# Delta rule and MLP on one core: chunks 2 and 3 from 32-token rows, and TensorE's small products regrouped

## The chip, the cores and the metric

The kernel runs on one core of a Trainium2 chip. The metric is the device time of one execution in microseconds (us), the median of three runs for the kernel before. A profiled execution gives a trace of every engine: TensorE (PE, with its weight loads PEld), VectorE (DVE), ScalarE (ACT), GpSimd (POOL) and SyncE (SP), and of the DMA queues. All inputs and results are fp32, but for the two weight matrices, which lie in DRAM as 64-bit numbers and are converted on the core.

## What is computed

A delta-rule attention over 4 batches, 8 heads, 768 tokens and head size 48, followed by layer norm and a two-layer MLP with a residual:

```python
def _attn_ref(q, k, v, beta):
    k_n = k / (np.linalg.norm(k, axis=-1, keepdims=True) + 1e-06)
    state = np.zeros((B, H, D, D)); y = np.zeros_like(q)
    for t in range(S):
        kt, vt, bt = k_n[:, :, t], v[:, :, t], beta[:, :, t, None]
        y[:, :, t] = np.einsum('bhd,bhde->bhe', q[:, :, t], state)
        v_old = np.einsum('bhde,bhd->bhe', state, kt)
        state = state + bt[..., None] * np.einsum('bhd,bhe->bhde', kt, vt - v_old)
    return y

def _moe_ref(x, g_ln, w_ch1, w_ch2):        # x: (4, 768, 384)
    mu, var = mean(x), mean((x - mu) ** 2)
    xn = (x - mu) / np.sqrt(var + 1e-06) * g_ln
    return x + np.maximum(xn @ w_ch1, 0.0) @ w_ch2    # 384 -> 1536 -> 384
```

## The kernel before

**Chunks.** The 768 tokens are cut into 12 chunks of 64 (`C`), and each chunk treats all 32 pairs of batch and head at once: two batches' halves on the partitions (`e`), heads in the columns. For a chunk the kernel forms the keys turned (`first_kt` by TensorE transposes, or `load_blocks` and `turned`, a DMA in blocks and a VectorE transpose), the Gram matrix of the keys (`gram`, or `gram_queries` together with the products of keys and queries), the inverse of a unit triangular matrix made from it and beta, and then `recur`: `ks` and `qs` (state times keys and queries), `u` (the inverse applied to v minus `ks`), the state's update `s`, the output `y`, layer norm, and x turned to `xnt` for the MLP.

**Inverses.** VectorE inverts by rows: step j multiplies a column by a row and subtracts (two instructions for each j). `rows_near` does this for blocks of 16 tokens (15 steps): once for chunk 0 alone and once for chunks 1 and 2 together, `rows_near((1, 2))`. From two 16-token blocks `near_join` makes the inverse of a 32-token block (two groups of TensorE products, E and Z, with copies between), and `join` makes the inverse of all 64 tokens from two of 32 (again two groups, e and z). So u of chunks 0, 1 and 2 is one product with a 64-token inverse (L1147, L1177). From chunk 3 `rows_inverse(m)` inverts 32-token blocks on VectorE (31 steps, L1058 and L1065) for the pair of chunks 2m+1 and 2m+2 (3 and 4 first), and u is formed in three steps (L1166): the first 32 tokens' inverse on v, the off-diagonal block of the Gram matrix (`goff`) on that u, subtracted from v on VectorE (L1170), and the second inverse.

**MLP.** `mlp(c)` multiplies chunk c's 256 rows with the two weight matrices. Chunks 0 to 2 use plain products for the first layer (L1447), chunk 0 also for the second (L1469); the others use sums of blocks that need fewer products (`eleven` with L1380 and sums on VectorE, `seven` with L1548 and sums on GpSimd). These products are the large ones; all others above are small and come in groups of 32 or 64.

**Buffers.** The eight banks of PSUM are `two` and `by` (two banks each, for the small products) and `f0` to `f3` (the MLP; at the start also the small ones). Chunk 0's and 1's q, gram and joins use several buffers of their own (`kt3`, `qt1`, `xn1`, `xt1`).

**Order.** All instructions are first entered as steps with an engine, an estimated cost and their inputs. `Line.schedule` plays the program through with these costs, picks for each engine the next step by priority (due times `DUE`, caps `CAP`, earliest times `T0`), and `emit` writes the instructions in the order of the planned starts, which `in_this_order` fixes for each engine and for the DMA issues. So a change of a cost or of these tables moves the whole order. `pe_time` holds what the plan believes of TensorE: a pass's cost (`PASS`), a cost for going between large and small products (`SWITCH`), 128 passes per block of instructions (`BLOCK`, `FETCH`), and a clock that depends on earlier windows (`WINDOW`, `WARM`). `warm_up` puts products with zeros (L1632) into TensorE's planned idle time until the MLP begins.

Of the kernel before, what the change touches and what calls it, by code (L numbers as in the profile page):

```python
# [65 lines left out]
PASS = 0.0165  # L66


class Step:
    __slots__ = (  # L70
        "eng", "cost", "fn", "deps", "pr", "lag", "bulk", "start", "end", "n", "users", "name", "t0", "np", "arr", "hold", "ready", "least", "due", "port", "banks", "cap", "pk"
# [3 lines left out]
class Line:  # L75
# [6 lines left out]
    PE_TAIL, SWITCH, OVERLAP = 0.12, 0.1, 0.1  # L82
    BLOCK, FIRST, FETCH = 128, 93, 3.95
    WINDOW, WARM, KEEP = 3.413, 0.44, 0.6
    DMA_ISSUE, DMA_DONE, LANES = 1.4, 1.0, 8

    def __init__(self):
        self.steps = []
        self.filler, self.fill_after, self.fills = None, (), []
        self.writer = {}  # L90
        self.readers = {}

    def add(self, eng, cost, fn, r=(), w=(), pr=0.0, lag=0.0, bulk=None, name="", t0=0.7, after=(), np=0, arr=0.0, hold=None, due=None, port=0, cap=None, pk=16.0):
        s = Step()
        s.eng, s.cost, s.fn, s.pr, s.lag, s.bulk, s.name, s.t0 = eng, cost, fn, pr, lag, bulk, name, t0
        s.np, s.arr, s.n = np, arr, len(self.steps)
        s.hold, s.due, s.cap, s.pk = False, due, cap, pk
# [15 lines left out]
        deps.discard(s)  # L113
        s.deps = sorted(deps, key=lambda d: d.n)
# [9 lines left out]

    def pe_time(self, s, t, commit):
        passes, bi, begun, wins = self.passes, self.block, self.begun, self.wins
        if self.big != (s.due is not None):
            t += self.SWITCH
        left, stall, new = max(s.np, 1), 0.0, {}
        per = s.cost / left  # L130
        while left:
# [9 lines left out]
            warm = wins.get(w - 1, 0.0) + new.get(w - 1, 0.0) >= self.WARM * self.WINDOW  # L141
            f = 1.0 if warm else 2.0
# [3 lines left out]
            new[w] = new.get(w, 0.0) + m * per  # L146
            t += m * max(per, f * min(per, self.wide(s)))
            passes += m
            left -= m
        if commit:  # L150
            self.big = s.due is not None
            self.passes, self.block, self.begun = passes, bi, begun
            for w, a in new.items():
                wins[w] = wins.get(w, 0.0) + a
        return t, stall

    def warm_up(self, t, until):
# [3 lines left out]
        while t + cost + 0.2 < until:  # L161
            w = int(t / self.WINDOW)
            if self.wins.get(w, 0.0) > self.KEEP * (t + cost - w * self.WINDOW):
                t = t + 0.1
                continue
# [47 lines left out]
    def offer(self, u):  # L213
        t = u.t0
        for d in u.deps:
            t = max(t, d.end + (self.NEXT if d.eng == u.eng and d.bulk is None else self.HOP))
        u.ready = t + u.lag
        self.avail[u.eng].append((u.ready, u))

    def foresee(self, now):  # L220

        soon, ends = {e: [] for e in ENGS}, {}
        for s in self.held:
# [5 lines left out]
            for d in s.deps:  # L229
                z = d.end if d.end is not None else ends.get(d, max(now, self.free[d.eng]) + d.cost)  # L230
                t = max(t, z + (self.NEXT if d.eng == s.eng and d.bulk is None else self.HOP))
# [4 lines left out]
    def run(self):  # L236
# [3 lines left out]
        self.passes, self.block, self.begun, self.wins = 0, 0, 0.7, {}  # L240
        self.big = False
# [42 lines left out]
        while todo:  # L284
# [29 lines left out]
            if any(r < t and h.start is None and h.pr < pick.pr for r, h in self.soon[e]):  # L314
                self.foresee(t)
            first = [max(r, t + 0.05) for r, h in self.soon[e] if h.start is None and h.pr < pick.pr]
            if first and t + pick.cost > first[0] + self.GIVE and waits.get(e, 0) < self.PATIENCE:
# [26 lines left out]
            if e == "PE":  # L344
                if self.filler and not self.big and self.fill_after and all(x.start is not None and x.end <= free[e] for x in self.fill_after):
                    self.warm_up(free[e], t)
# [14 lines left out]
    def schedule(self):  # L361
# [5 lines left out]
        for s in reversed(every):  # L367
# [4 lines left out]
            if s.due is None:  # L372
                s.pr -= self.EAGER * (s.eng == "PE")
        goal = min((s for s in every if s.due is not None), key=lambda s: s.due)
# [28 lines left out]
def kernel(  # L403
# [23 lines left out]
    NSL = (NCH - 1 + SLAB - 1) // SLAB  # L427
# [5 lines left out]
    NP = H // 2  # L433
    TURNED = 4
    LNPE = 2
# [9 lines left out]
    def sb(name, shape, dt=FP32):  # L445
# [21 lines left out]
    xn1, xt1 = sb("xn1", [128, GH, C]), sb("xt1", [128, GH, C])  # L467
    kts = [kq[:, 0] for kq in kqs] + [sb("kt3", [128, GH, C])]
    qts = [kqs[0][:, 1], sb("qt1", [128, GH, C]), kqs[1][:, 1], kqs[2][:, 1]]
    pts = [sb(f"pt{i}", [128, GH, C]) for i in range(2)] + [xn1, xt1]  # L470
# [3 lines left out]
    xts = [xt0, xt1, kqs[1][:, 1], xt3]  # L474
# [10 lines left out]
    xnjs = [  # L485
        t.rearrange("p h t -> p (h t)").rearrange("p (c h t) -> p c h t", c=SLAB, t=BK) for t in (kqs[2][:, 1], xn1)
    ]
# [8 lines left out]
    xor, bits, ma, mb_ = (small[:, n].bitcast(I32) for n in range(4))  # L496
    mask4 = sb("mask4", [128, BK], I32)
    lane = sb("lane", [128, 3])
    beta_s = sb("beta_s", [128, 1 + SLAB, FB])
# [5 lines left out]
    second = [t.rearrange("p h t -> p (h t)") for t in (qts[1], pts[1])]  # L505
# [5 lines left out]
    knrm = sb("knrm", [128, GH])  # L511
# [3 lines left out]
    two = psum.tile([128, 2, 512], FP32, name="two")  # L515
    by = psum.tile([128, 2, 512], FP32, name="by")
    f_ = [psum.tile([128, 512], FP32, name=f"f{i}") for i in range(4)]
# [3 lines left out]
    DUE = [427.765, 583.601, 213.154, 268.307, 795.608, 269, 907.321, 333.938, 602.225, 394.884, 1217.56, 1460.55, 0.099, 0, 1.793, 59.617]  # L521
    CAP = [700.448, 198.32, 1075.41, 558.357, 371.457, 461.226, 203.442, 537.048, 455.27, 590.32, 447.02, 315.018, 444.4, 322.431, 447.17, 466.169, 726.277]
    T0 = [18.636, 10.706, 30.485, 64.109, 123.03, 38.361, 76.47, 154.521, 173.066, 81.563, 50.167, 32.713, 40.943, 38.356, 19.795, 25.96, 3.78, 24.511, 36.996, 21.431, 91.901, 74.05]
# [18 lines left out]
    def one_of(c):  # L542

        return c % 2 if c < 3 else (0, 0, 2, 3)[c - 3 if c < 4 else 1 + (c - 4) % 3]

    def kt_of(c):
        return c if c < 4 else (c - 4) % 3
# [18 lines left out]
    def dma(eng, out_, in_, n, ns, r=(), w=(), **kw):  # L566

        cost = 0.65 if eng == "Pool" else 0.39 if ns == 115 else 0.68 if ns in (16.5, 16) else 0.46 if ns == 168 else 0.62 if n < 128 else 0.53
# [13 lines left out]
    for i in (2, 1):  # L582
        c_dve(
            lambda i=i: nc.vector.memset(tb[i].rearrange("p (h d) -> p h d", d=DP)[:, :, D:], 0.0), 0.28, [("tbpad", i)],
        )
# [17 lines left out]
    )  # L603
    c_dve(lambda: nc.vector.tensor_copy(out=lane[:, 1:2], in_=ma[:, 0:1]), 0.1, [("lane", 1)], ["ma"], port=2)
# [3 lines left out]
    )  # L608
    c_dve(
# [3 lines left out]
    SMALL = ["xor", "bits", "ma", "mb"]  # L613
# [17 lines left out]
    def load_padded(i, src, c, engs, **kw):  # L631
        for e in range(2):
# [5 lines left out]
    def load_v(c, **kw):  # L638
        for e in range(2):
            dma("SP", vs[c % NV][half(e)], nat(v, c, e), GH * C, 16.5, w=[("v", c % NV, e)], **kw)  # L640

    def load_raw(c, engs=("SP", "SP"), dst=None, keys=None, **kw):

# [10 lines left out]
    def load_blocks(i, src, c, eng, **kw):  # L654
        dst = tb[i].rearrange("p (h u d) -> p h u d", u=2, d=BK)
# [37 lines left out]
    def fetch(i, **kw):  # L693
        dst = words[BUF[i]].rearrange("p n w -> p (n w)")
# [3 lines left out]
        dma("ACT", dst, src, 256, 115, w=WORD_KEYS[BUF[i]], **kw)  # L698

    def convert(i, c0=0, n=WN, **kw):  # L700

# [42 lines left out]
    def first_kt(src, skeys, dst, dkey, pair, **kw):  # L744
        for g in range(2):
# [11 lines left out]

    def scale_v(c, kn, kk, **kw):
        vk = [("v", c % NV, e) for e in range(2)]
# [3 lines left out]
                out=vs[c % NV], in0=vs[c % NV], in1=kn[:, :, None].to_broadcast([128, GH, D]), op=ALU.mult  # L763
# [6 lines left out]
    def turned(c, i, dst, dkey, **kw):  # L770
        was = {("qt", 2): [(n, x, *y) for x in (1, 2) for n, y in (("gn", ()), ("gnx", (0,)), ("gnx", (1,)))], ("qt", 3): [("xn", 0), ("xn", 1)]}
# [983 lines left out]
```

## Time and profile before

| | us |
|---|---|
| median of 3 runs (540.9, 537.87, 539.72) | 539.72 |
| the profiled execution | 537.88 |
| its span, first to last instruction | 536.0 |
| chunk 0's x copied out of PSUM (L1222) | 48.64 |
| first product of the MLP (L1447) | 69.1 |
| last product of TensorE | 531.2 |

The span is what the trace shows; the execution's own time is 1.9 us longer. The views read are the page (busy time per engine, then 40 slices of the span with a digit for each tenth of busy time), the busy time of each engine in stretches, each engine's instructions in order of time, the groups of instructions by line, and the chain of work that ended last. A record such as `L1166 x64` is one group of 32 products of the code, since the trace has two records for each. An idle time's cause stands in brackets; "issue" means that the engine waited for nothing that the profile shows.

The largest groups of TensorE (busy us, records):

| line | what | records | busy us |
|---|---|---|---|
| L1548 | MLP second layer, `seven` | 924 | 219.2 summed by form |
| L1380 | MLP first layer, `eleven` | 1188 | 172.9 summed by form |
| L1447, L1469 | MLP, plain products | 264 | 69.1 |
| L1166 | u in three steps, chunks 3 to 11 | 1728 | 23.8 |
| L883 | `gram_queries`, chunks 5 to 11 | 896 | 16.2 |
| L808 | `gram`, chunks 0 to 4 | 640 | 9.5 |
| L1020 | `near_join`, chunks 0 to 2 | 768 | 9.3 |
| L1087, L1093 | `join`, chunks 0 to 2 | 384 | 5.0 |
| L1632, L740 | products with zeros | 58 | 21.4 |

The large products' busy times are sums over forms that overlap, so they exceed TensorE's 509.6 us when added up.

### The profile page before, as it was taken

Reading aid. Unit: us, or ns where it says so; the run is one execution under the profiler, and the core shown is the slowest. Engines: PE = TensorE matmul, PEld = TensorE weight load, DVE = VectorE, ACT = ScalarE, POOL = GpSimd, SP = SyncE. Lnnn points to the kernel's source line nnn. Section 1 sums busy time; section 2 is a strip of 40 time slices with the busy share of each in tenths; the row PEclk is TensorE's granted clock in tenths of the full one; section 3 lists DMA queues with packets and bytes.
Section 4 is the critical chain, followed back from the end, with each engine's and each line's share of the span. In section 5 each row is a group of like instructions: output and inputs, shape, how many; then the busy total and the mean of one; then the engine's idle time right before and its main releaser. Section 6 shows DMA issues by size and latency. Waiting matters only on the chain.

```text
span 536.0 us, 23353 instructions
## 1 busy us (share of the span) xinstructions
PE 509.6 (95%) x10308; PEld 458.9 (86%) x10308; DVE 385.2 (72%) x898; ACT 195.1 (36%) x476; POOL 216.5 (40%) x322
## 2 busy tenths in 40 slices
PE   6778789999999989999999999999999999999996
PEld 3657678667888879999999999999989999999996
DVE  2779967897299878538979938979889889244331
ACT  3657766424502223442431434332223313222220
POOL 5120851114355553154351343273452542624442
PEclk8979799999999999999999999999999999999999
DMA  9775835736233766632631063301112101111101
GB/s 163 142 186 151 219 88 104 129 59 122 34 52 53 125 98 117 106 58 35 125 54 32 10 126 93 77 2 32 42 37 74 33 17 34 43 32 53 38 2 29
DMA packets 155861, 40.55 MB, mean 76 GB/s; under 512 B 149232, under 2 KB 152304, under 8 KB 155760
## 3 DMA queue, kind: packets, MB, share of 16 engines
q1 hardware_dynamic: 151920, 29.41, 31.2%
q10 hardware_dynamic: 3552, 9.63, 5.4%
q8 instruction: 80, 1.31, 1.0%
q14 instruction: 21, 0.17, 0.1%
q0 software_dynamic: 288, 0.03, 0.1%
HBM read 30.79 MB, written 8.26 MB: 73 GB/s over the span
## 4 chain that ended last, share of the span: by engine, by line
PE 79%; DVE 11%; SPq 4%; issue 3%; DMA 2%; ACT 0%; DVEq 0%; ACTq 0%
PE f L1548 28%; PE f L1380 22%; PE f L1447 7%; SPq L569 4%; PE f L1469 3%; PE two L1166 3%; PE two L883 3%; PE two L1130 2%; PE by L1130 2%; PE f L1020 2%; PE by L1184 2%; PE f L1632 2%; DVE tmp L1058 1%; PE two L1194 1%; DVE xb L1065 1%
## 5 line engine op out<-in xcount | busy, mean ns | idle before, releaser
L1534 POOL TENSOR_TENSOR h_all<-h_all 128x256 f32<-128x256 f32 x99 | 74.3, 756 | 66.1 <-PE f L1548 54.5
L1548 PE MATMUL f<-w_sb,h_all 128*128 128x192 f32 x396 | 96.5, 332 | 0.8 <-DVE o L1566 0.7
L1548 PE MATMUL f<-words,h_all 128*128 128x192 f32 x396 | 90.9, 329 | 0.0
L1380 PE MATMUL f<-xnt,w_sb 128*128 128x128 f32 x648 | 89.1, 277 | 0.5 <-DVE h_all L1402 0.3
L1380 PEld LDWEIGHTS f<-xnt,w_sb 128*128 128x128 f32 x648 | 80.8, 192 | 1.8 <-DVE h_all L1402 0.8
L1573 POOL TENSOR_TENSOR words<-h_all 128x128 f32<-128x128 f32 x66 | 32.6, 509 | 114.2 <-ACT h_all L1399 98.1
L1402 DVE TENSOR_TENSOR h_all<-f,h_all 128x256 f32<-128x256 f32 x135 | 56.1, 422 | 25.4 <-PE f L1380 15.9
L1548 PEld LDWEIGHTS f<-w_sb,h_all 128*128 128x128 f32 x396 | 66.1, 190 | 4.1 <-issue 1.6
L1548 PEld LDWEIGHTS f<-words,h_all 128*128 128x128 f32 x396 | 67.8, 190 | 1.1 <-DVE tmp L1058 0.2
L1065 DVE TENSOR_TENSOR xb<-xb,tmp 128x31 f32<-128x31 f32 (+15 forms) x155 | 61.7, 398 | 4.2
L1058 DVE TENSOR_TENSOR tmp<-xb,gb 128x31 f32<-128x31 f32 (+15 forms) x155 | 61.9, 399 | 3.8
L1447 PE MATMUL f<-xnt,w_sb 128*128 128x256 f32 x216 | 51.3, 385 | 0.0
L1447 PEld LDWEIGHTS f<-xnt,w_sb 128*128 128x128 f32 x216 | 39.8, 190 | 5.9 <-issue 0.4
L1399 ACT ACTIVATE h_all<-f 128x256 f32<-128x256 f32 x54 | 20.7, 384 | 54.2 <-PE f L1380 34.2
L1548 PE MATMUL f<-w_sb,words 128*128 128x192 f32 x132 | 31.8, 329 | 0.0
L1399 ACT ACTIVATE h_all<-h_all 128x256 f32<-128x256 f32 x54 | 22.2, 415 | 25.4 <-DVE h_all L1402 25.2
L1566 DVE TENSOR_TENSOR o<-f,x 128x192 f32<-128x192 f32 x33 | 11.6, 352 | 27.4 <-PE f L1548 22.9
L894 ACT COPY gdiag<-two 64x128 f32<-64x128 f32 (+1 forms) x42 | 16.1, 382 | 31.9 <-DVE pt L897 12.4
L1456 ACT ACTIVATE h_all<-f 128x256 f32<-128x256 f32 x36 | 13.6, 385 | 37.6 <-PE f L1447 37.3
L762 POOL TENSOR_TENSOR v<-v,knrms 128x768 f32<-128x768 f32 x11 | 18.1, 1647 | 20.5 <-DVE knrms L1005 9.6
L1222 ACT COPY x<-by 128x384 f32<-128x384 f32 x23 | 10.7, 482 | 37.9 <-DVE o L1566 29.1
L1172 ACT COPY u<-two 128x768 f32<-128x768 f32 x18 | 14.4, 798 | 27.5 <-PE two L1166 27.2
(222 smaller groups left out, 915.3 us busy)
## 6 DMA issues: line engine op xcount, KB each, us to landing
words<-in_moe_w_ch_dram ACTq DMA_DIRECT2D x8, 768.0 KB, 5.2
v<-in_v_dram SPq DMA_DIRECT2D x24, 192.0 KB, 4.6
out_dram<-o SPq DMA_DIRECT2D x48, 96.0 KB, 2.2
kr<-in_k_dram SPq DMA_DIRECT2D x46, 96.0 KB, 3.4
xld<-xlt SPq DMA_DIRECT2D x9, 384.0 KB, 2.4
xnt<-xld SPq DMA_DIRECT2D x36, 96.0 KB, 3.1
tb<-in_q_dram SPq DMA_DIRECT2D x40, 64.0 KB, 3.0
tb<-in_k_dram SPq DMA_DIRECT2D x32, 64.0 KB, 3.2
```

The source lines that it names most:

```text
L569: add(eng, cost, lambda: QUEUE[eng].dma_start(out=out_, in_=in_), r, w, bulk=n * ns / 16e3, pk=ns, **kw)
L762: lambda: nc.gpsimd.tensor_tensor(out=vs[c % NV], in0=vs[c % NV], in1=kn[:, :, None].to_broadcast([128, GH, D]), op=ALU.mult),
L1058: lambda j=j, n=n, w=w, t=t: nc.vector.tensor_tensor(out=t, in0=xb[:, 0:n, j : j + 1].to_broadcast([128, n, w]), in1=gb[:, j : j + 1, j + ...
L1065: "DVE", dve(n * w), lambda t=t, rest=rest: nc.vector.tensor_tensor(out=rest, in0=rest, in1=t, op=ALU.subtract),
L1130: nc.tensor.matmul(dst[half(e), hp, j], src[drows(hp), (e if n else key_half(c, hp, e)) * GP + j], s_all[drows(hp), e, j], start=(n == 0 o ...
L1380: nc.tensor.matmul(wide(p[:, 128 * n : 128 * n + 128]), w[:, f : f + 128], r, start=start and n == 0, stop=stop, skip_group_check=True)
L1399: add("ACT", act(256), lambda: nc.scalar.activation(to[0], p, ACTF.Relu), pk, to[1])
L1402: add("DVE", dve(256), lambda: nc.vector.tensor_tensor(out=to[0], in0=ps(p), in1=y[0], op=op), [*pk, *y[1]], to[1])
L1447: nc.tensor.matmul(p[:, 0:TOK], w1_sb[:, t, f * 128 : (f + 1) * 128], xnt[:, t], start=(t == 0), stop=(t == KC - 1))
L1534: add(eng, cost, lambda: e.tensor_tensor(out=out_, in0=x, in1=y, op=op), r, w, port=2 if eng == "Pool" else 1, pr=-2)
L1548: lambda f=f, t=start and f == 0: nc.tensor.matmul(p[:, 0:D2], lhs(f), rhs[:, f], start=t, stop=(f == F2 - 1), skip_group_check=True),
L1573: lambda f=f + i: e.tensor_tensor(out=s3[f], in0=one(0, 0)[0](f), in1=one(1, 0)[0](f), op=ALU.subtract),
```

## The change

- Only chunks 0 and 1 start from 16-token blocks (`NEAR` 3 becomes 2), each alone: `gram_near(c)` makes the Gram matrix in 64 passes of 64x64 (before: 128 of 64x32 and 32x32), VectorE transposes it from PSUM, and four masked sums pick the 16-token blocks. `near_join` stays for them, with one PSUM bank in place of two; `join` is gone, and so are the 64-token inverses.
- Chunks 0, 1 and 2 form u in three steps as the others do.
- `rows_inverse(m)` now serves chunks 2m and 2m+1, so the first serves 2 and 3. `gram` (64 passes of 64x64) makes the Gram matrices of chunks 2 and 3; from chunk 4 on `gram_queries` makes both products (before from chunk 5).
- `gram_queries` puts its first half into `two` and its second into `by`, the second right behind the first; in the second block of each product 64 columns go through in place of 128. `qs` stands behind the second step of u, `y` behind `s` (`gate`).
- beta for the 16-token blocks is loaded as whole rows of 128 values and selected on VectorE; the loads of chunk keys, weights and beta have new earliest times.
- The plan has other costs (`PASS`, `SWITCH` and `DRAIN`, `STAY`, `WARM` and `COLD`), stays with small products when the next one is ready within 0.2 us, ends the products with zeros for good at the first large product, and has a table `OFF` of priority offsets, one for each part of the program. `HOOKS` is empty, so nothing hangs on it.

```diff
-PASS = 0.0165
+PASS = 0.0155
...
-    PE_TAIL, SWITCH, OVERLAP = 0.12, 0.1, 0.1
+    PE_TAIL, SWITCH, DRAIN, STAY, OVERLAP = 0.12, 0.19, 0.09, 0.2, 0.1
...
+            stay = None
+            if e == "PE" and not self.big and pick.due is not None:
+                for rd, s in self.avail[e]:
+                    if s.due is None:
+                        x = when(s, e, rd)
+                        if x is not None and x <= t + self.STAY and (stay is None or (x, s.pr, s.n) < stay[0]):
+                            stay = (x, s.pr, s.n), s
+                if stay is not None:
+                    t, pick = stay[0][0], stay[1]
...
-                if self.filler and not self.big and self.fill_after and all(x.start is not None and x.end <= free[e] for x in self.fill_after):
+                if self.filler and not self.late and self.fill_after and all(x.start is not None and x.end <= free[e] for x in self.fill_after):
...
+    NEAR = 2
+    NSL = (NCH - NEAR) // SLAB
...
+    def gram(c, pair, **kw):
...
+        def prod():
+            for x in range(GP):
+                for hp, e in hp_e:
+                    f = (2 * key_half(c, hp, e) * NP + x % NP + x // NP * NP) * C
+                    nc.tensor.matmul(g[half(e), hp, x * C : x * C + C], flat[drows(hp), f : f + C], flat[drows(hp), f : f + C])
...
+    def gram_near(c, n, **kw):
...
+        pe(64, prod, [("kt", kt_of(c), x) for x in range(2)], pk, 0.86, per=0.0157, name=f"G{c}", **kw)
+        got = add(
+            "DVE", 1.24,
+            lambda: nc.vector.transpose(
+                gb.rearrange("p s t -> p (s t)").rearrange("p (t x h) -> p t x h", x=4, h=GH), g.rearrange("p (h x t) -> p t x h", h=GH, x=4)
+            ),
+            pk, ["gb"], **kw,
+        )
...
+                add(
+                    "DVE", dve(256),
+                    lambda v=v, m=m: nc.vector.scalar_tensor_tensor(out=g16, in0=v, scalar=m, in1=g16, op0=ALU.mult, op1=ALU.add),
+                    ["gb", ("lane", 2 + n)], [gk], port=1, **kw,
+                )
...
+                        w, f, x = C - b * BK, lk + b * BK, lq - lk + GH * C
+                        o = ps[quad(2 * (e ^ hp) + b), hp, j * 2 * C : (j + 1) * 2 * C]
+                        nc.tensor.matmul(
+                            segs(o, 96, BK) if b else o, flat[drows(hp), f : f + BK], segs(flat[drows(hp), f : f + 1], x, w),
+                        )
...
+    def gram_queries(c, **kw):
+        line.part += 1
+        made = gram_half(c, 0, two, TWO, **kw)
+        gram_half(c, 1, by, BY, gate=made, **dict(kw, lag=0.0))
...
-        chunks = [c for c in (2 * m + 1, 2 * m + 2) if c < NCH]
+        chunks = (2 * m, 2 * m + 1)
...
-    def join(c, **kw):
...
-        elif c:
-            def prod_u():
...
+            last = pe(64, prod_u, r, TWO, 0.16, per=0.0113, name=f"u{c}", **(dict(cap=cap(c + 5)) if c else {}), **kp_e)
+            if n == 1:
+                if c:
+                    pe(64, lambda: state(p_y, qt, 1), qtk + ["s_all"], [*BY, "qs"], 0.65, name=f"qs{c}", gate=last, **kw)
+                add("DVE", dve(768), lambda: nc.vector.tensor_tensor(out=v_j, in0=v_j, in1=p_2, op=ALU.subtract), TWO, vk, **kw)
...
-    rows_near((1, 2))
...
+    rows_near((1,))
...
+    near_join(1)
+    first_kt(tb[2], keys, kts[0], ("kt", 0), PAIRS[0])
+    gram(3, PAIRS[0])
+    rows_inverse(1)
+    step(1)
+    prep_q(2, t0=T0[23])
     mlp(0)
     differences("DVE", dve(F2 * D2))
-    rows_inverse(1)
-    for c in range(2, NCH):
+    step(2)
+    mlp(1)
+    prep_q(3, t0=T0[24])
+    for c in (4, 5):
+        prep_gq(c)
+    rows_inverse(2)
+    step(3)
+    mlp(2)
+    prep_gq(6)
+    for c in range(4, NCH):
         step(c)
         mlp(c - 1)
...
+        if c + 3 < NCH:
+            prep_gq(c + 3)
+            if c % 2 == 0 and c + 3 not in HOOKS:
+                rows_inverse((c + 3) // SLAB)
```

## The prediction

> **What bounds the kernel now.** I read the page's busy table and 40 slices first, then the busy time by stretches, TensorE's instructions in order of time, and the chain that ended last. From the page:
>
> ```profile
> span 536.0 us, 23353 instructions
> PE 509.6 (95%) x10308; PEld 458.9 (86%) x10308; DVE 385.2 (72%) x898; ACT 195.1 (36%) x476; POOL 216.5 (40%) x322
> PE   6778789999999989999999999999999999999996
> PEclk8979799999999999999999999999999999999999
> DMA  9775835736233766632631063301112101111101
> ```
>
> TensorE is busy 95% of the span; its clock is down only in the first six slices, where DMA is busiest. The busy time by stretches cuts the span at the first MLP product (69.1), at 124.7 and at TensorE's last product (531.2); the columns are stretch, length, busy time per engine, clock, DMA share, GB/s:
>
> ```profile
> 69.10:124.70 55.60, 53.08 (x1535) 39.74 (x1535) 45.84 (x99) 28.11 (x63) 15.78 (x13) 1.00 0.50 97
> 124.70:531.20 406.50, 403.37 (x7191) 378.76 (x7189) 289.81 (x666) 125.14 (x331) 173.70 (x268) 1.00 0.29 57
> 0.00:69.10 69.10, 53.14 (x1585) 40.39 (x1585) 49.18 (x133) 41.88 (x83) 26.98 (x42) 0.85 0.78 168
> ```
>
> From 69.1 to 531.2, 462.1 us, TensorE idles 5.6 us. The time is therefore two things: when the first MLP product can start, and how much TensorE has to do afterwards; 4.8 us of output follow. In the first stretch 53 us look busy, but 21.4 of them are products with zeros (L740 4.71, L1632 16.71). TensorE in order of time there (start, length, line, count, idle before):
>
> ```profile
> 22.52 1.57 PE L1632 MATMUL f<-u 128*128 128x256 f32 x6
> 24.03 1.27 PE L808 MATMUL by<-kq 48*32 48x64 f32 x109
> 27.52 0.35 PE L808 MATMUL by<-kq 48*32 48x64 f32 x19 [2.21 <-issue]
> ...
> 60.89 0.67 PE L1130 MATMUL two<-s_all,kq 48*64 48x48 f32 x12 [2.96 <-issue]
> ```
>
> "issue" is a wait for nothing the profile shows. These waits come every 128 products (here 13+6+109 since the previous one) and add up to 11.9 us over the waits that TensorE's products show, the last at 106. VectorE in the same way shows what the start waits for and when the first 32-token inversion runs:
>
> ```profile
> 52.44 0.98 DVE L1228 BATCH_NORM_STATS2 st<-x 128x6 f32<-128x384 f32 x2
> ...
> 69.95 1.25 DVE L1037 STREAM_TRANSPOSE gb<-gdiag 128x1024 f32<-128x1024 f32 x1 [2.51 <-ACT gdiag L829]
> ...
> 116.67 2.10 DVE L1070 STREAM_TRANSPOSE xt<-xb 128x1024 f32<-128x1024 f32 x1
> ```
>
> Chunk 0's x is copied out by 48.64, yet its first MLP product comes at 69.1. The chain shows what a change of kind costs TensorE later:
>
> ```profile
> 214.80 0.81 PE two L1166 x64
> 215.61 2.43 PE f L1380 x20
> ...
> 369.13 12.96 PE f L1380 x116
> ```
>
> Undisturbed, an MLP record of L1380 takes 12.96/116 = 0.1117 us; the 20 after a small group take 2.43, not 2.23. Each visit to small products costs 0.19 us beyond the products. I count 81 visits after 69.1. (The records hold two per product of the code; "x64" is one group of 32.)
>
> **The change, products.** Removed, by rows summed over the span: five 128-record grams, L808 9.51; chunk 2's near_join, a third of L1020's 9.30, 3.10; all joins, L1087 2.46 and L1093 2.56; the one-step u of chunks 0 to 2, L1147 1.32 and L1177 2.30; one queries group, L846 1.16. Sum 22.4. Added: four 64-record grams (gram_near 0 and 1, gram 2 and 3), same shape as L846, 6.32/5 = 1.26 each, 5.0; chunk 4 through gram_queries, two groups at 16.2/14 = 1.16, 2.3; three u steps for three chunks, nine groups at (15.9+7.9)/27 = 0.88, 7.9. Sum 15.3, net **-7.1**. The narrower second block in gram_half (128 moving columns become 64) I take at nothing: 64-record groups of 64x128, 48x64 and 48x48 all cost 1.08 to 1.09 in the chain. It could give 0.2 on each of 16 groups, -3, if columns did set it.
>
> **Visits.** The halves of gram_queries now follow each other (two, then by), and qs follows the second u step. Alone today: 13 halves, 9 qs, some 4 joins and near_joins; 8 paired halves stay, and chunks 1 and 2 add four u visits. That is 17 to 18 fewer of 81, at 0.19: **-3.2**. Bounds: 0, if the planned order spreads them again, and -5 at 0.28 (y right behind s takes 0.93 where y alone takes 1.08, which adds 0.15 to the 0.1 on the way out). The Trainium skill, "TensorEngine Tiling (Array Packing)", section Key Properties, speaks against half of this: changing the tiling mode drains the engine, and u (32x32) to qs (48x64) changes it, so only the halves would gain; by it the visits are worth about -2.3. No row of before has qs behind u.
>
> **The start.** Chunk 0's path by today's rows. Keys copied at 11.2, unchanged. Gram 1.16 (L846): 12.4. VectorE's transpose straight from PSUM at the 1024-element price 1.25, in place of L824's copies: 13.8 with a hop. Four selections, 0.35 + 3 x 0.48: 15.7. Root to first step 2.3, inversion 7.1, expansion 1.9: 27.0. Transpose 0.7, E and Z at 1.9 to 2, copy 0.6, predicated copy 0.7, hops: 33.3; the second transpose and the whole join (38.05 to 44.4 today) are gone. In their place three u steps: 3 x 0.9 on TensorE, 2 x 0.80 on ScalarE, 0.93 on VectorE, six hops of 0.2: 39.7. y and copies 1.4: 41.1, against 48.64. From there LN (3.4), transposes (1.7) and scaling (1.5) make 47.7 unobstructed. Today these 6.6 us take 20.5: VectorE does chunks 1 and 2's expansion first (3.8), TensorE has the 2.96 wait, cold zeros 2.7, then a gram and qs (3.6) before the first product. Chunk 1's inversion is now alone (ops of 0.2, not 0.29), 1585 records before the first product become some 860, and the first half of w1 is issued at once. I keep some 4 of the 14 us of obstruction: **first MLP product at 52**. Bounds: 46 (nothing in the way, and E, Z without their waits) and 62 (all 14 kept).
>
> The Trainium skill, "Runtime: NRT & Kernel Launch", section Instruction fetch mechanics, says that instruction blocks of 256 are fetched ahead and that crossing one is mostly hidden. 128 products with their 128 weight loads are such a block, and the trace differs: 11.9 us of waits fall there. By the page fewer early products would free nothing and the start would be some 3 us later.
>
> **The sum.** After the first product, before: 462.1. What moves behind it: q1's and k3's transposes 2.2, ks1 and qs1 2.2, grams 2 and 3 2.5, chunk 4 jointly 1.2. What leaves there: E2, Z2 2.8, joins 1 and 2 3.3, L1177 2.3, against six u groups 5.3. Net +5.0; visits -3.2: 463.9. So 52 + 463.9 + 4.8 = 520.7 span, and 1.9 around it (537.88 against 536.0): 522.6. The profiled run is 1.8 below the median 539.72 (runs 537.87 to 540.9); I add half: **523.5**.
>
> Edits costed at nothing: gdiag and goff copies on ScalarE (36% busy; uncovered 0.6 each); VectorE's three extra v subtractions (0.93 each) against fewer transposes; 8 beta loads of 128-float rows plus four selections of 0.14 to 0.5 on VectorE, in its idle time before 15; k3 through tb[2] as before; weights issued earlier on ScalarE's queue, behind which k0's two loads stand first: if they delay k0, each us goes on the start one for one, inside 46 to 62. The second gram half sits in by, behind the x copy that empties it; covered by MLP products planned in between (L1222 waited 7.3 us on TensorE in all, without holding it).
>
> **Rivals.** (1) *Late start*, 0.25: DMA is 0.78 busy to 69.1, and early weights and chunk loads compete; the start stays at 62 or beyond and only the removed work shows: 62 + 463.9 + 6.7 = 532.6, less 2 because waiting TensorE does small work first: 530. For it: DMA slices at 9 and 7. Against: by 43.5 four weight pieces had been sent for, and Pool idles from 36 to 53.
>
> (2) *Slower: the pair inversion for chunks 2 and 3 comes late*, 0.12. Today the first 32-token inversion serves chunk 3 and ends at 118.8, 48.8 us after 69.95, though its own work is some 24. It now has to serve chunk 2. MLP(2) would be wanted at 52 + (158.3 - 69.1) = 141; from inverse to its input I reckon 20, so 121 is the point; started at 60 it ends at 109. Past 121 each us is lost, and VectorE (72%) has every later pair due one chunk earlier too. Twenty us past (at 141), or 5 at each of four pairs, and the time is 543 or more.
>
> (3) *The change does not do what it says*, 0.07: small groups are not joined and the start gains as forecast: 527.
>
> **Chances.** Forecast (515 to 528) 0.56, with rivals (1) 0.25, (2) 0.12, (3) 0.07. Of (1) a few hundredths end near 537 or above. Half a per cent (2.7 us) is about what can be told from no change. Faster 0.83, same 0.04, slower 0.13. The range is 512 (start 46, fewer visits at -5) to 537, where (1) fades out.
>
> **What would show it.** First L1469-type and MLP first-layer products at 46 to 56; 17 fewer visits; TensorE's records down 576 apart from zeros; issue waits below 8 us; idle after the first product still about 6. Wrong, if TensorE waits for VectorE's inversion in the 100 to 150 stretch, or the first MLP product is past 60.

## The result, and the profile after

The changed kernel takes **874.1 us** (median of 4 runs, 861.38 to 879.49) where the kernel before takes 539.12 (537.87 to 540.9) beside it: a ratio of **1.609, 95% interval 1.588 to 1.630**. Executions show two states, and the ratio goes by the faster one alone, in which the changed kernel ran twice (861.38 and 873.73, 867.6 us in the middle). The profile is of an execution of 874.47 us. Forecast were 523.5 us and a range of 512 to 537. The prediction was wrong in sign, and the change in time is some twenty times the one it foresaw.

The page of the kernel after, in four of the lines that were shown of the kernel before (busy time per engine, then 40 slices):

```profile
span 872.8 us, 22164 instructions
PE 683.5 (78%) x9710; PEld 561.5 (64%) x9710; DVE 383.0 (44%) x909; ACT 190.5 (22%) x454; POOL 209.3 (24%) x316
PE   5767889898788866788778788977877897777776
PEclk7868999899968999958999656975675578568559
```

VectorE, ScalarE and GpSimd are busy as long as before, to some 7 us. TensorE has 598 records fewer and is busy 174 us longer, and where the slices stood at 9 from the seventh on (but for one at 8 and the last), most now stand at 7 or 8. So this is not a late start: the whole MLP part is stretched. The busy time from the first MLP product (75.04) to about TensorE's end, after and then before (stretch, length, busy time of PE, PEld, DVE, ACT, POOL, clock, DMA share, GB/s):

```profile
75.00:868.00 793.00, 635.04 (x8470) 525.71 (x8468) 335.77 (x764) 151.55 (x385) 184.13 (x278) 0.80 0.18 35
```

```profile
69.03:531.20 462.17, 456.52 (x8731) 418.57 (x8724) 335.65 (x764) 153.32 (x394) 189.55 (x281) 1.00 0.32 62
```

With 261 records fewer, that part takes 331 us longer: TensorE's idle time there goes from 5.7 to 158.0 us (+152), and the records themselves from 456.5 to 635.0 (+178), at a granted clock of 0.80 in place of 1.00. The costliest group of the MLP's first layer, from the groups of instructions, after and before (busy us, mean ns of one, idle us before it and what ended most of it):

```profile
L1418 PE MATMUL f<-xnt,w_sb 128*128 128x128 f32 x648 | 146.0, 375 | 53.3 <-DVE h_all L1440 25.1 <-ACT h_all L1437 14.6 <-DVE h_all L1453 10.1
```

```profile
L1380 PE MATMUL f<-xnt,w_sb 128*128 128x128 f32 x648 | 89.1, 277 | 0.5 <-DVE h_all L1402 0.3
```

The same 648 records wait 53.3 us in place of 0.5, mostly for VectorE (25.1 and 10.1) and for ScalarE (14.6). And these two wait for TensorE. Four lines of the list of waits of the kernel after (us in total, times, longest):

```profile
DVE h_all L1440 <- PE f L1418: 197.8, 106, 7.7
ACT h_all L1437 <- PE f L1418: 151.4, 36, 12.7
DVE o L1607 <- PE f L1589: 80.1, 33, 11.2
PEld f L1418 <- DVE h_all L1440: 76.2, 95, 1.3
```

Engines that wait for each other take turns. How, is seen in the instructions in order of time; TensorE after:

```profile
801.74 0.52 PE L1589 MATMUL f<-w_sb,h_all 128*128 128x192 f32 x1
802.78 1.23 PE L1418 MATMUL f<-second,q_last 128*128 128x128 f32 x4 [0.51 <-DVE h_all L1453]
804.52 2.07 PE L1418 MATMUL f<-xnt,w_sb 128*128 128x128 f32 x8 [0.52 <-DVE o L1607]
807.12 1.23 PE L1418 MATMUL f<-ident,second 128*128 128x128 f32 x4 [0.52 <-ACT h_all L1437]
```

and VectorE in the same stretch:

```profile
802.30 0.42 DVE L1453 TENSOR_TENSOR h_all<-h_all,f 128x256 f32<-128x256 f32 x1 [1.00 <-PE f L1589]
804.11 0.36 DVE L1607 TENSOR_TENSOR o<-f,o 128x192 f32<-128x192 f32 x1 [1.39 <-PE f L1418]
```

L1607 reads what the second layer's L1589 has written, in the written-out program bank 2 of the four that the MLP has, and L1589's last product ended at 802.26. Yet L1607 starts at 804.11, when the four records of L1418 have ended, which write bank 1. And the eight records that follow start at 804.52, 0.05 us after L1607 has ended, though they write banks 3 and 0 and need nothing of it. Before, a like stretch is closed:

```profile
504.65 0.61 PE L1380 MATMUL f<-pt,q_last 128*128 128x128 f32 x4
505.10 0.61 PE L1380 MATMUL f<-xnt,w_sb 128*128 128x128 f32 x4
505.55 0.61 PE L1380 MATMUL f<-ident,pt 128*128 128x128 f32 x4
```

Four records take 0.61 us there and overlap their followers, which start 0.45 us behind them; after, four take 1.23 and stand alone. Two things are mixed in this 1.23: from 802.5 to 812 the granted clock is 0.50, where the stretch of the kernel before has 1.00. Elsewhere in the kernel after the clock is 1.00 (218 to 240), and there the next group comes at 237.69:

```profile
236.46 0.71 PE L1418 MATMUL f<-second,w_sb 128*128 128x128 f32 x4 [0.59 <-DVE h_all L1440]
```

So at full clock a group behind a gap takes 0.71, and groups that take turns come every 1.23 us in place of every 0.45; the low clock comes on top.

These lines of the diff do it. Neither the list of changes nor the forecast spoke of them:

```diff
-    two = psum.tile([128, 2, 512], FP32, name="two")
-    by = psum.tile([128, 2, 512], FP32, name="by")
-    f_ = [psum.tile([128, 512], FP32, name=f"f{i}") for i in range(4)]
+    t4, f4 = (psum.tile([128, 4, 512], FP32, name=n) for n in ("t4", "f4"))
+    two, by = t4[:, 0:2], t4[:, 2:4]
+    f_ = [f4[:, i] for i in range(4)]
```

The eight banks of PSUM are the same; but they are now two tiles of four banks where they were six. `gram_near` can so take two neighbouring banks out of one tile. In the written-out programs I counted the waits on other engines by what is awaited. "Other bank" means that the two instructions share only the tile. Waits that also bring TensorE an input are left out:

| | kernel before | after | split (e1) | tiles of two banks (e5) |
|---|---|---|---|---|
| TensorE waits for a reader of the bank that it writes | 325 | 23 | 302 | 99 |
| TensorE waits for a reader of another bank of the tile | 16 | 291 | 10 | 173 |
| a reader waits for the writer of the bank that it reads | 427 | 61 | 436 | 222 |
| a reader waits for a later writer of another bank | 9 | 350 | 12 | 171 |

So in these programs the waits follow the tile and not the bank. Theory A, to be tested: these waits are the loss. Rivals: the new order of work (B), and the low clock by itself (C).

### The profile page after: what moved, and what is told of

Read it like the earlier page. It is cut to its first block, busy times and chain, and to the rows that moved or that the text cites. A ratio compares the mean times of both kernels' runs of the same rounds, so it can differ in the third digit from the quotient of the medians.

```text
span 872.8 us, 22164 instructions
## 1 busy us (share of the span) xinstructions
PE 683.5 (78%) x9710; PEld 561.5 (64%) x9710; DVE 383.0 (44%) x909; ACT 190.5 (22%) x454; POOL 209.3 (24%) x316
## 4 chain that ended last, share of the span: by engine, by line
PE 67%; DVE 17%; ACT 8%; issue 5%; DMA 2%; POOL 0%; DVEq 0%; ACTq 0%; SPq 0%; POOLq 0%
PE f L1418 29%; PE f L1589 19%; DVE h_all L1440 6%; PE f L1486 6%; PE t L1204 4%; PE t L1174 3%; ACT h_all L1437 2%; DVE o L1607 2%; DVE tmp L1133 2%; PE t L969 2%; PE t L1219 1%; DVE xb L1140 1%; DVE h_all L1453 1%; PE t L1229 1%; PE f L1508 1%
## 5 line engine op out<-in xcount | busy, mean ns | idle before, releaser
L1418 PE MATMUL f<-xnt,w_sb 128*128 128x128 f32 x648 | 146.0, 375 | 53.3 <-DVE h_all L1440 25.1
L1418 PEld LDWEIGHTS f<-xnt,w_sb 128*128 128x128 f32 x648 | 119.1, 263 | 78.3 <-DVE h_all L1440 36.2
L1589 PE MATMUL f<-w_sb,h_all 128*128 128x192 f32 x396 | 111.5, 372 | 17.3 <-DVE o L1607 5.0
L1589 PE MATMUL f<-words,h_all 128*128 128x192 f32 x396 | 104.0, 365 | 16.3 <-ACT words L1620 7.3
L1589 PEld LDWEIGHTS f<-w_sb,h_all 128*128 128x128 f32 x396 | 74.6, 212 | 29.2 <-DVE o L1607 7.4
L1589 PEld LDWEIGHTS f<-words,h_all 128*128 128x128 f32 x396 | 74.2, 210 | 25.0 <-DVE o L1607 6.9
L1418 PE MATMUL f<-second,w_sb 128*128 128x128 f32 x216 | 50.9, 375 | 22.7 <-DVE h_all L1440 14.1
L1437 ACT ACTIVATE h_all<-f 128x256 f32<-128x256 f32 x54 | 20.7, 385 | 186.5 <-PE f L1418 151.4
L1418 PEld LDWEIGHTS f<-second,w_sb 128*128 128x128 f32 x216 | 40.3, 260 | 32.6 <-DVE h_all L1440 19.8
L1486 PEld LDWEIGHTS f<-xnt,w_sb 128*128 128x128 f32 x216 | 40.0, 194 | 20.3 <-ACT h_all L1495 10.8
L1607 DVE TENSOR_TENSOR o<-f,x 128x192 f32<-128x192 f32 x33 | 11.7, 356 | 72.3 <-PE f L1589 65.3
L1589 PE MATMUL f<-w_sb,words 128*128 128x192 f32 x132 | 33.2, 336 | 6.5 <-DVE o L1607 6.5
L1418 PE MATMUL f<-second,q_last 128*128 128x128 f32 x108 | 26.4, 386 | 12.4 <-DVE h_all L1440 8.9
L1214 ACT COPY u<-t 128x768 f32<-128x768 f32 x24 | 19.2, 798 | 69.1 <-PE t L1204 60.5
L1418 PE MATMUL f<-ident,second 128*128 128x128 f32 x108 | 26.1, 384 | 8.6 <-DVE h_all L1440 4.7
```

The source lines that it names most:

```text
L1418: nc.tensor.matmul(wide(p[:, 128 * n : 128 * n + 128]), w[:, f : f + 128], r, start=start and n == 0, stop=stop, skip_group_check=True)
L1437: add("ACT", act(256), lambda: nc.scalar.activation(to[0], p, ACTF.Relu), pk, to[1])
L1486: nc.tensor.matmul(p[:, 0:TOK], w1_sb[:, t, f * 128 : (f + 1) * 128], xnt[:, t], start=(t == 0), stop=(t == KC - 1))
L1589: lambda f=f, t=start and f == 0: nc.tensor.matmul(p[:, 0:D2], lhs(f), rhs[:, f], start=t, stop=(f == F2 - 1), skip_group_check=True),
L1607: lambda: e.tensor_tensor(out=out_, in0=a, in1=b_, op=ALU.add), r, w, pr=pr,
```

## The experiments

**Tiles of PSUM, four kernels on one chip beside the kernel before (535.24 us).** First the changed kernel with six tiles again; the order of the work is the same:

```diff
-    t4, f4 = (psum.tile([128, 4, 512], FP32, name=n) for n in ("t4", "f4"))
-    two, by = t4[:, 0:2], t4[:, 2:4]
-    f_ = [f4[:, i] for i in range(4)]
+    two, by = (psum.tile([128, 2, 512], FP32, name=n) for n in ("two", "by"))
+    f_ = [psum.tile([128, 512], FP32, name=f"f{i}") for i in range(4)]
...
-        bank, pk = ((t4, TWO), (t4, BY), (f4, FK[0] + FK[1]), (f4, FK[2] + FK[3]))[n]
+        bank, pk = ((two, TWO), (by, BY))[n]
```

> The changed kernel with its eight PSUM banks as six tiles again (two, by, f0 to f3), as before the change; order and work are the changed kernel's. Theory A (the two four-bank tiles tie TensorE to readers of banks it does not write): TensorE's idle time after the first MLP product falls from about 170 us to under 15, the clock there goes back to 1.00, and the time to 515 to 535, near the forecast of 523.5. Theory B (the newly planned order itself does not fit the chip, products stand right behind the reads they need): the time stays above 800. Theory C (the clock is what fell, because the products with zeros stop earlier): the time stays above 750 with a clock near 0.8.

Measured: 542.32 us, ratio 1.013 (1.008 to 1.018). The page and the same group of the split kernel:

```profile
span 539.1 us, 22161 instructions
PE 504.1 (94%) x9710; PEld 455.7 (85%) x9710; DVE 387.3 (72%) x909; ACT 189.4 (35%) x454; POOL 211.5 (39%) x316
PEclk8595879999999999999999999999999999999999
L1417 PE MATMUL f<-xnt,w_sb 128*128 128x128 f32 x648 | 89.1, 278 | 2.2 <-DVE h_all L1439 0.9 <-ACT xnt L1303 0.7 <-DVE o L1606 0.5
```

The waits are gone (53.3 to 2.2 us), a record takes 278 ns again, and the clock is back at full from the seventh slice on. Nothing was done to the clock, so it had followed the gaps: C falls as a cause of its own. The order is the changed one, so B falls too. The time lies above the 515 to 535 that was expected of theory A; the rest is taken up below. Next, only one of the two tiles split:

```diff
 # e2: f0 to f3 apart, t4 as one tile
-    t4, f4 = (psum.tile([128, 4, 512], FP32, name=n) for n in ("t4", "f4"))
+    t4 = psum.tile([128, 4, 512], FP32, name="t4")
-    f_ = [f4[:, i] for i in range(4)]
+    f_ = [psum.tile([128, 512], FP32, name=f"f{i}") for i in range(4)]
 # e3: two and by apart, f4 as one tile
-    two, by = t4[:, 0:2], t4[:, 2:4]
+    two, by = (psum.tile([128, 2, 512], FP32, name=n) for n in ("two", "by"))
```

> The changed kernel with f0 to f3 as four tiles; two and by stay one tile t4. Theory A, with most of the waits in the MLP's banks: 525 to 590. Theories B and C: above 750.

> The changed kernel with two and by as tiles of their own; f0 to f3 stay one tile f4. Theory A: still 780 to 870, since the MLP's products are those that wait most (L1418 lost 53 us idle before its products in the changed kernel's groups). Theories B and C: no change, 860 to 880.

Measured: 562.12 us (1.049, 1.042 to 1.056) with the small products' tile shared, 853.52 (1.593, 1.583 to 1.604) with the MLP's tile shared. Against the split kernel that is +20 and +311, in sum 331, and the kernel after, timed beside another run of the kernel before, has some +325 (867.6): the two add up, and 94% of their sum is the MLP's tile. Then the merge alone, on the kernel before:

```diff
-    two = psum.tile([128, 2, 512], FP32, name="two")
-    by = psum.tile([128, 2, 512], FP32, name="by")
-    f_ = [psum.tile([128, 512], FP32, name=f"f{i}") for i in range(4)]
+    t4, f4 = (psum.tile([128, 4, 512], FP32, name=n) for n in ("t4", "f4"))
+    two, by = t4[:, 0:2], t4[:, 2:4]
+    f_ = [f4[:, i] for i in range(4)]
```

> The kernel before with its eight banks as two tiles of four, nothing else changed. Theory A: 800 to 900, the whole loss without the rest of the change. Theory B: 535 to 545. Theory C: 535 to 560, since its products with zeros are as before.

Measured: 816.09 us, ratio 1.523 (1.509 to 1.538), with nothing else changed; the clock falls here too, to 0.895 over the span (0.979 before). Its groups show the pattern:

```profile
L1380 PE MATMUL f<-xnt,w_sb 128*128 128x128 f32 x648 | 122.1, 328 | 47.2 <-DVE h_all L1402 20.2 <-ACT h_all L1399 13.4 <-DVE h_all L1415 8.2
```

So theory A is shown from both sides: taking the merge out of the changed kernel removes the loss, and putting it into the kernel before makes one of the same kind.

**Half the sharing.** `f0` and `f1` in one tile of two banks, `f2` and `f3` in another, `two` and `by` apart:

```diff
-    f_ = [psum.tile([128, 512], FP32, name=f"f{i}") for i in range(4)]
+    ff = [psum.tile([128, 2, 512], FP32, name=n) for n in ("f01", "f23")]
+    f_ = [ff[i // 2][:, i % 2] for i in range(4)]
```

> The split kernel with the MLP's four banks as two tiles of two banks (f0 with f1, f2 with f3). Theory A, with the loss set by how many of TensorE's waits name a reader of another bank: in the written-out program these are 173 here against 10 in the split kernel and 274 with the four banks in one tile (ratio 0.62), so 542 + 0.62 x 311 = 735, taken as 650 to 790. Rival: only sharing one tile among all four banks of the MLP's rotation costs, since with two tiles TensorE has another tile to go to: below 600.

Measured: 586.03 us, ratio 1.093 (1.086 to 1.100). My proportional reckoning missed: the program has 173 and 171 waits on other banks, more than half of the 274 and 317 with four banks in one tile (e3), but the loss is 44 us and not half of 311, as the rival in the expectation had it. Both parts of the loss are smaller: TensorE idles 50 us of the span (35 in the split kernel, 176 in e3) and is busy 532.6 (504.1 and 675.5), and the clock stays at full from the seventh slice on, where e3 has 0.797 over its span. Why so few of the waits cost anything I read so, without a run that shows it: as long as TensorE can write one tile while the readers empty the other, most of these waits end before anyone stands at them; with all four banks in one tile the MLP has no second one.

**What remains: the split kernel is not faster than before.** Split, the kernel takes 542.3 us (540.75 to 543.37) where I had forecast 523.5. Its stretch from the first MLP product (68.98) to TensorE's end (534.2) is 465.2 us, the forecast 463.9; so nearly all that is missing, 17 us, lies ahead of it. The start was forecast to shrink to 52, and it stays at 69. Lines of TensorE of the split kernel there:

```profile
9.90 1.94 PE L800 MATMUL by<-ident,kr 128*128 128x128 f32 x8 [4.03 <-DMA kr<-in_k_dram]
46.55 0.86 PE L1203 MATMUL two<-v,xt 32*32 32x48 f32 x32 [2.32 <-issue]
47.34 2.08 PE L1669 MATMUL f<-u 128*128 128x256 f32 x4
52.49 2.07 PE L1669 MATMUL f<-u 128*128 128x256 f32 x4
65.13 0.77 PE L1094 MATMUL f<-xt,xne 32*32 32x32 f32 x66 [2.81 <-issue]
68.58 0.47 PE L850 MATMUL two<-kq 48*64 48x64 f32 x2 [1.23 <-issue]
```

and ScalarE at the last step of u:

```profile
49.45 0.80 ACT L1213 COPY u<-two 128x768 f32<-128x768 f32 x1 [1.84 <-PE f L1669]
```

The products with zeros (L1669) read their zeros from columns of the buffer named `us`, so the copy of u waits until they have ended. That gave three experiments: the zeros in a buffer of their own, no zeros, and the first weights fetched later (the last two let the plan make a new order). They ran beside a kernel before of 536.81 us.

```diff
 # e6, in the same order
-    nought, small = us.rearrange("p h d -> p (h d)")[:, 0:128], ...
+    nought, small = os_[0][:, 0:128], ...
 # e7
-    line.filler = (zeros, 0.44, "f0")
+    line.filler = None
 # e8: T0[10], T0[11], T0[12] and T0[21]
-0.700001, 0.7000011, 3.54484681681, ... 0.904770757952
+20.0, 20.0, 20.0, ... 20.0
```

> The split kernel with the zeros for TensorE's filling products in the first 128 columns of o0, idle until the MLP's end, instead of in u's buffer; the order of all engines is the same. In the split kernel the first MLP product came at 69.0, not at the forecast's 52. Theory S1 (filling products stand on chunk 0's path, because u's copies wait for the products that read the zeros in u's buffer, and the products then wait for the copies): chunk 0's second half of x is copied out 3 to 5 us earlier than 57.6, and the time falls by 1 to 4 to 538 to 541. Theory S2 (waits for TensorE's instructions and the slow clock set the start): within 1 of the split kernel.

> The split kernel without the filling products (the order is planned again without them). Theory S1: chunk 0's path is freed as in the run with zeros of their own, 538 to 541, if the clock does not fall further. Theory S2: the clock to 69 us falls below the 0.74 it has now, products there take twice as long, first MLP product at 71 or later, 543 to 548.

> The split kernel with the four weight pieces that are sent for in the first 6 us held back to 20 us in the plan. Theory S3 (these loads delay chunk 0's keys and the fetching of TensorE's instructions): first key products at 8.4 in place of 9.9, waits that no profile row explains down from 10.9 us to under 7, time down 2 to 6 to 536 to 540. Rival (loads do not set the start; conversions of late weights do): first MLP product no earlier than 69, time 542 to 550.

Measured: 541.18 us with the zeros apart (ratio 1.006, 1.002 to 1.010; first MLP product 66.71, 2.3 us earlier, and the second half of x copied out at 54.70 for 57.64), 592.97 without zeros (1.104, 1.097 to 1.111), 565.81 with late weights (1.056, 1.050 to 1.062). With late weights the first MLP product does come at 61.51, 7.5 us earlier. What is lost comes later: from the first MLP product to TensorE's end the kernel with late weights takes 36 us longer than the split one, 18.8 of them in a single wait (L1417 for VectorE's L1606), and the one without zeros 58 us longer, with a longest wait of 20.6 at the same place. So the zeros apart gave about what was expected of S1 (in time within the noise: the ratios 1.006 and 1.013 have intervals that overlap), and the other two times lie outside all that was expected. In both the plan made another order from tables that belong to one order, so these two tell nothing of the zeros or the weights by themselves. I therefore repeated the question with the order kept. In e9 only the second and third weight fetch and the arithmetic on them stand 9 us further down; in e10 three gaps of TensorE's start get more products with zeros, within the steps that stand before them; e11 has both and the zeros apart; e12 has e10 and the zeros apart.

```diff
 # e9: a shift in emit, after the plan is made
+        at = {}
+        for s in sorted(self.steps, key=lambda s: (s.start, s.n)):
+            at[s] = max([s.start + self.moved.get(s, 0.0)] + [at[d] for d in s.deps])
-        for s in sorted(self.steps, key=lambda s: (s.start, s.n)):
+        for s in sorted(self.steps, key=lambda s: (at[s], s.start, s.n)):
             s.fn()
...
+        if i in (1, 2):
+            line.moved[line.steps[-1]] = 9.0
 # e10: behind chunk 0's Gram products; the same behind chunk 1's transposes,
 # and one product more behind the first zeros
+            if c == 0:
+                for _ in range(4):
+                    zeros()
```

> The kernel with six separate PSUM tiles (541 to 542 us, first MLP product at 68.98 us in its profile), with the second and third weight fetch and the arithmetic on what they bring 9 us further down in the written order; TensorE's order is untouched. In the split kernel 2.56 MB of weights and only 0.79 MB of keys and queries moved in the first 16 us (before the change 0.98 and 1.48 MB), and chunk 0's key transposes began at 9.90 instead of 8.36 us. Theory T1 (the weight fetches ahead of the keys make the start late): the key transposes come at about 8.4 us, chunk 1's at about 14 instead of 16.3, the first MLP product 1.5 to 4 us earlier (65 to 67.5), total 537.5 to 540. Rival T2 (the cold TensorE and its waits for instructions decide): the transposes come earlier but the first MLP product stays within 1 us of 69, total 540 to 543.

> The split kernel with nothing moved, and more products of zeros in three gaps of TensorE's start: one product of 128x512 more ahead of chunk 0's key transposes, four of 128x256 behind chunk 0's Gram products and four behind chunk 1's key transposes. In the split kernel the granted clock from 13.4 to 26.8 us was 0.50 (before the change 0.92) and eight key transposes took 1.94 us there (before 1.09). T2 (clock): the granted clock of that stretch rises above 0.75, the transposes take about 1.1 us, the inversion of chunk 0 starts about 1 us earlier, the first MLP product comes 1 to 4 us earlier (65 to 68), total 538 to 541. T1 (weight fetches): the clock rises but the first MLP product stays at 68.5 to 69.5, total 541 to 543.

> The split kernel with both edits (weights further down, more zeros products in the gaps) and the zeros held in a buffer of their own. If the start's causes add up: first MLP product at 61 to 65 us, total 533 to 538, level with or below the kernel before the change (about 536). If something else holds the start (the waits for instructions, or the chain on VectorE): first MLP product at 66 us or later, total 538 to 542.

> The split kernel with the additional zeros products in the gaps of the start and the zeros in a buffer of their own; the weight fetches stay where they were. With the weights moved as well the first MLP product came at 65.5 us and then TensorE waited 5.5 us for converted weights; without that move the wait should be gone. If the early weights cost the start little: first MLP product at 64.5 to 67.5 us, no wait above 2 us for w_sb, total 533 to 538, level with the kernel before. If what the moved weights gave was needed for the 65.5: first MLP product at 68 us or later and a total of 539 to 544.

Measured, e9 to e11 beside 540.18 us and e12 beside 537.21: 549.67 (1.020, 1.014 to 1.025), 545.32 (1.012, 1.005 to 1.018), 547.02 (1.014, 1.008 to 1.020), 543.13 (1.010, 1.006 to 1.013). No kernel that was run is faster than the one before. The times of e9, e10 and e11 lie above all that was expected of them, in part because the kernel before is some 3 us slower beside them too: by its ratio e10 is level with the split kernel's 1.013. e12 is in its second range. Lines of TensorE of e9:

```profile
8.80 1.94 PE L804 MATMUL by<-ident,kr 128*128 128x128 f32 x8 [2.95 <-DMA kr<-in_k_dram]
13.33 1.97 PE L804 MATMUL f<-ident,kr 128*128 128x128 f32 x8
70.72 1.22 PE L1489 MATMUL f<-xnt,w_sb 128*128 128x256 f32 x2
77.46 6.66 PE L1489 MATMUL f<-xnt,w_sb 128*128 128x256 f32 x16 [5.53 <-POOL w_sb L780]
```

The keys do come earlier without the weights in front: chunk 1's at 13.33 for 16.31 (16.62 in e6), so the weights had delayed these; chunk 0's at 8.80 for 9.90, which is less sure, since e6 has 9.08 with the weights in front. But the first MLP product comes at 70.72, and then converted weights are missing for 5.53 us: a new wait in place of the old one. In e11, with all three edits, the first MLP product does come at 65.54, and two records later TensorE waits 5.49 us for the same weights, until 72.25. The busy time of e12 in the cold stretch, and TensorE behind it:

```profile
13.40:26.80 13.40, 10.29 (x170) 8.13 (x168) 12.19 (x44) 10.34 (x22) 2.88 (x4) 1.00 1.12 206
```

```profile
30.57 1.93 PE L1100 MATMUL f<-xne,second 32*32 32x32 f32 x128 [4.42 <-DVE xne L1095]
```

With more zeros the clock of this stretch goes from 0.50 to 1.00 (e10: 0.86, and eight transposes take 1.04 us for 1.94). But the first product of the inverse comes at 30.57 for 31.17, because it waits 4.42 us for VectorE, and the first MLP product at 68.10 for 68.98. Nor is that small gain the warm clock's: the zeros apart alone (e6) have 30.42 and 66.71 at a clock of 0.63, and more zeros alone (e10) have their first MLP product at 70.71:

```profile
70.71 6.38 PE L1491 MATMUL f<-xnt,w_sb 128*128 128x256 f32 x18
```

Neither the weights nor the clock by itself, then, brings the start forward in this order, and what the added zeros cost behind 31 us was not followed up. Up to 31 it is VectorE's chain that TensorE waits for in e12; from there to 69 it is the steps of the next table together, and which of them alone would give most was not settled.

## Why the prediction was wrong, point by point

**The step that failed: the sum had no term for the tiles of PSUM.** It costed every group of instructions that goes or comes, and took from the stretch behind the first MLP product (462.1 us, 5.6 idle) that TensorE would go on without gaps. That rests on banks that are written and read in turn, each free of the others, and the diff took just this away. "Edits costed at nothing" does not list the three lines. They cost some 325 us. The Trainium skill, "Perfetto Trace Analysis", section Optimizing Tensor Performance, says that independent groups of products should go round through the banks, so that one is emptied while the next is written. The kernel after does go round (banks 1, 3 and 0 in the lines above), and the overlap is lost all the same; by these runs it takes banks in tiles of their own. None of the rivals holds it: the slower one put the loss into VectorE's inversion for chunks 2 and 3, in a single stretch after 121 us.

**The first MLP product at 52: mis-sized, even without the merge.** The split kernel has 68.98. By the steps of the forecast:

| step of chunk 0, end at | forecast us | split kernel us | lost in this step |
|---|---|---|---|
| inversion and expansion | 27.0 | 28.91 | 1.9 |
| E, Z and the predicated copy | 33.3 | 37.75 | 2.5 |
| u in three steps | 39.7 | 50.25 | 6.1 |
| y, s and the copies of x | 41.1 | 57.64 | 6.0 |
| first MLP product | 52 | 68.98 | 0.4 |

Most of it (12.1 of 17.0 us) lies in u, y and s. I costed them at bare durations with six hops, whereas the path has two issue waits (1.24 and 2.32), two lots of zeros at a low clock (2.08 and 2.07), the copy of u behind such zeros, and s planned ahead of the second half of y. The first three kinds were to be seen in the kernel before (there the copy of u, L1151, waits 1.42 us for zeros); that y stands behind s is in the list of changes. I counted them as obstruction only behind x, where I kept 4 of 14 us; that part held (11.3 for 10.9). The keys are 1.75 us late (copied by 12.95, forecast "unchanged" 11.2): for chunk 1 e9 shows that the early weights delay them, for chunk 0 it is likely; the text named this, and the sum priced it at nothing. Ahead of the first MLP product stand 1241 records and not the 860 I reckoned, since chunk 1's E and Z and queries were planned there.

**Issue waits below 8 us: wrong.** The split kernel has 10.9 us of them (before 11.9), in spite of 598 records less. The forecast had weighed the Trainium skill, "Runtime: NRT & Kernel Launch", section Instruction fetch mechanics, by which crossing a block is mostly hidden. These runs disagree with it in the start: 2.32, 2.81 and 1.23 us stand in the lines above.

**The work behind the first MLP product: right.** Forecast 463.9, split kernel 465.2, idle 8.5 for "about 6". TensorE's records without the zeros fall by 576, as forecast (10250 to 9674). Visits to small products go from 80 to 68 by the written order, 12 fewer where I said 17. What is saved and what is moved behind balance out, as the sum had it; the gain was to come from the start alone, and did not come. The rule that a change of tiling mode drains TensorE (the Trainium skill, "TensorEngine Tiling (Array Packing)", section Key Properties) was not tried by itself in any run.

**The rivals.** "Late start", 62 or beyond and 530 us, is what the split kernel does, only later (69) and so at 542.3. VectorE's inversion for chunks 2 and 3 holds nothing up: in the split kernel TensorE is busy 49.99 of the 50 us from 70 to 120 and all of the 40 behind them.

## What to carry to other kernels

A line that only renames or regroups buffers can change the dependencies; ask of every tile who reads one part while another is written, and cost that as a wait of each on the other. When TensorE and its readers each show the other as the cause of their waits, and every product group stands alone, look at what they share before looking at the order. Where an order is planned from tables, vary one thing with the order kept, or the new order is what gets measured (565.81 and 592.97 us here, against 541 to 550 with the order kept).

## What the runs showed that I had not expected

- Taking turns costs more than the gaps: in the kernel after TensorE idles 152 us more, and its records take 178 us more beside that, at a clock of 0.80. Four records behind a gap of 0.5 us took 0.71 at full clock and 1.23 at a clock of 0.50, where a closed run brings four every 0.45.
- Sharing costs much more when no second tile is left: +44 us with two banks to a tile, +311 with four, for a count of waits that is not even double.
- A warm TensorE brought nothing here: with the clock between 13.4 and 26.8 us at 0.86 in place of 0.50 the first MLP product came 1.7 us later (e10 against the split kernel), and at 1.00 in place of 0.63 it came 1.4 us later (e12 against e6). Each is one profile.
